# RMS-normed attention and a gated MLP on one core: tokens on 64 lanes of 7 in place of 112 of 4, q and k on the two halves of the partitions, keys in chunks of 128

## The chip, the cores and the metric

The kernel runs on one core of a Trainium2 chip. The time is the device time of one execution in microseconds (us). The core has five engines with a queue each: TensorE (PE in the profile), VectorE (DVE), ScalarE (ACT), GpSimd (POOL) and SyncE (SP, which here only issues transfers). Before the change the median was 428.67 us.

## The reference

```python
q_n, k_n = rmsnorm(q, g_q), rmsnorm(k, g_k)     # 8 batches x 12 heads x 448 tokens x 64
attn = softmax(q_n @ k_n.T / 8)                 # per head
x = (attn @ v).transpose(0, 2, 1, 3)            # -> 3584 tokens x 768
h = x @ w_in                                    # 768 x 2048
out = (h * sigmoid(1.702 * h)) @ w_out          # 2048 x 768
```

## The kernel before

Heads are worked in 48 pairs. For each pair q, k and v are loaded, q and k squared (ACT), summed (DVE), normed (POOL), transposed, scored against each other (TensorE), exponentiated (ACT), multiplied with v (TensorE) and divided (DVE). From the first batch on the two projections of the MLP run in between on TensorE.

In the cuts below "..." marks what is left out, and long names are shortened. The order on every engine is fixed before the run: a list scheduler gets each task with its engine, a planned duration and a priority, and writes out one queue for each engine; each queue then runs in the order written. The priorities of the first pairs were tuned against the planned durations.

```python
# loads: 112 partitions, 4 tokens each; one transfer for q, one for k, one for v
src = (q, k, v)[which][b, h0:h0 + 2].rearrange("h (ss ns) d -> ss h ns d", ns=NS)   # ss = 112
nc.sync.dma_start(out=vraw[turn(i, N_RAW, K_VRAW)][:SS], in_=src)                    # v
eng.dma_start(out=raw[turn(i, N_RAW, K_RAW)][:SS, which], in_=src)                   # q or k
...
# the scheduler's task for a load: 0.46 us of SyncE, 0.9 us of movement
od.add(("L", i, w), "SP", 460, lambda: load(i, w), at - 7 + ...,
       deps=[("N", prior(i, N_RAW, K_RAW), gi) for gi in range(2)], moves=900.0)
...
# scores: 4 chunks of 112 keys, two heads on the two halves of TensorE's rows
for hp in range(2):
    r = slice(64 * hp, 64 * hp + 64)
    nc.tensor.matmul(sc[:, hp, ...], lhsT=qkw[r, k0:k0 + WIN], rhs=qk[r, 0, qs])
# values: 4 matmuls of 65 columns for each head and block of queries
for kc in range(NS):
    nc.tensor.matmul(os_[u, w][:, x, :], lhsT=att[:SS, kc, hp, ...], rhs=vx[:SS, hp, kc, :])
```

## Time and profile before

| | before |
|---|---|
| time, median of 3 | 428.67 us (428.58 to 428.96) |
| span of the profiled run | 426.3 us |
| TensorE busy in the span | 96% |
| TensorE busy from 100 to 370 us | 265.0 of 270 us |
| SyncE: issuing loads, all told | 73.3 us for 143 loads |

The busy shares and the table by stretch are shown in the prediction below.

And two rows of the waits (who waited, for what: total us, times, longest):

```profile
DVE ssq L534 <- ACT sq L525: 9.8, 14, 3.8
ACT sq L525 <- DMA raw<-in_k_dram: 7.0, 7, 1.5
```

### The profile page before, as it was taken

The numbers are of one execution on the slowest core, as the hardware profiler recorded it, in microseconds if no ns is written. First come the engines' busy times: TensorE is split into PE (matmuls) and PEld (weight loads), VectorE is DVE, ScalarE is ACT, GpSimd is POOL, SyncE is SP. The second block draws the span as 40 slices with busy tenths as digits, with TensorE's granted clock in tenths as the row PEclk, the third lists the DMA queues.
The fourth block names the chain that finished last, engine by engine and source line by source line (L and its number), as shares of the span: only waits on it lengthen the run. The fifth ranks groups of instructions, "written<-read, shape, count | busy, mean of one in ns | idle before, by whom it ended". The sixth has DMA issues, their size and how long they took to land.

```text
span 426.3 us, 10048 instructions
## 1 busy us (share of the span) xinstructions
PE 409.1 (96%) x3874; PEld 241.7 (57%) x3874; DVE 297.3 (70%) x584; ACT 302.6 (71%) x437; POOL 189.8 (45%) x277
## 2 busy tenths in 40 slices
PE   6899899999989999999999999999999999999995
PEld 4558686655555555555555555555555555565553
DVE  5967988579988677965787577764676555655663
ACT  4898788869978699978986589867775477604400
POOL 6396853657387473854636355553642100000000
PEclk9999999999999999999999999999999999999999
DMA  8999999575559989667636687556333630121023
GB/s 224 248 257 245 258 246 248 141 161 129 134 124 205 219 196 208 155 166 156 170 103 160 156 227 165 136 136 169 74 77 95 157 90 13 23 67 38 0 75 92
DMA packets 101555, 63.38 MB, mean 149 GB/s; under 512 B 54916, under 2 KB 101508, under 8 KB 101508
## 3 DMA queue, kind: packets, MB, share of 16 engines
q1 hardware_dynamic: 93712, 55.88, 53.9%
q0 software_dynamic: 7296, 6.29, 9.0%
q8 instruction: 30, 0.49, 0.5%
q10 hardware_dynamic: 500, 0.57, 0.4%
q14 instruction: 17, 0.14, 0.1%
HBM read 45.61 MB, written 11.01 MB: 133 GB/s over the span
## 4 chain that ended last, share of the span: by engine, by line
PE 78%; DVE 11%; ACT 5%; issue 3%; DMA 2%; POOL 0%; DVEq 0%
PE w L875 30%; PE w L965 17%; PE o L664 10%; PE sc L643 9%; PE sc L965 4%; PE w L905 4%; DVE late L956 4%; PE sc L875 2%; ACT att L653 2%; ACT sq L525 1%; DVE ssq L534 1%; DVE obs L675 1%; DVE g L897 1%; DMA raw<-in_k_dram 1%; DVE w_out_s L945 1%
## 5 line engine op out<-in xcount | busy, mean ns | idle before, releaser
L651 ACT ACTIVATE att<-sc 112x896 bf16<-112x896 f32 x168 | 145.8, 917 | 33.4 <-PE sc L643 32.9
L875 PE MATMUL w<-xt,w_in_s 128*128 128x448 bf16 (+1 forms) x810 | 150.7, 330 | 0.1
L875 PEld LDWEIGHTS <-w_in_s 128*128 128x128 bf16 x864 | 78.1, 97 | 54.2 <-issue 6.7
L576 POOL TENSOR_TENSOR row<-raw,rs 112x512 bf16<-112x512 f32 x80 | 89.5, 1139 | 25.8 <-DMA qk<-row 13.5
L664 PEld LDWEIGHTS <-att 112*128 112x128 bf16 x1536 | 72.5, 98 | 49.3 <-issue 18.2
L897 DVE SCALAR_TENSOR_TENSOR g<-th,w 128x448 bf16<-128x448 f32 x119 | 72.5, 616 | 26.8 <-ACT th L885 26.3
L885 ACT ACTIVATE th<-w 128x448 f32<-128x448 f32 x119 | 64.6, 548 | 26.3 <-PE w L875 24.7
L664 PE MATMUL o<-vx,att 112*128 112x65 bf16 x1280 | 74.2, 194 | 4.9 <-DVE obs L675 4.7
L589 POOL TENSOR_TENSOR vx<-vraw,ones 112x512 bf16<-112x512 f32 x35 | 36.5, 1042 | 95.0 <-PE o L664 59.4
L534 DVE TENSOR_REDUCE ssq<-sq 112x16 f32<-112x1024 f32 (+1 forms) x50 | 58.5, 1171 | 10.4 <-ACT sq L525 9.8
L525 ACT ACTIVATE sq<-raw 112x1024 f32<-112x1024 f32 (+1 forms) x43 | 44.5, 1036 | 11.2 <-DMA raw<-in_k_dram 7.0
L643 PE MATMUL sc<-qk 64*128 64x448 bf16 (+1 forms) x360 | 46.9, 342 | 1.6 <-DVE qk L606 1.4
L675 DVE TENSOR_TENSOR obs<-o,rcp 112x256 bf16<-112x256 f32 x96 | 40.8, 425 | 3.3
L965 PEld LDWEIGHTS <-g 128*128 128x128 bf16 x336 | 29.9, 97 | 19.6 <-issue 3.0
L674 DVE RECIPROCAL rcp<-o 112x4 f32<-112x4 f32 x96 | 17.1, 178 | 33.0 <-PE o L664 32.4
L965 PEld LDWEIGHTS <-late 128*128 128x128 bf16 x328 | 28.8, 97 | 18.3 <-issue 2.6
L965 PE MATMUL w<-w_out_s,g 128*128 128x384 bf16 x176 | 33.5, 325 | 0.0
L965 PE MATMUL w<-w_out_s,late 128*128 128x384 bf16 x152 | 29.7, 326 | 0.2 <-DVE late L956 0.2
L965 PE MATMUL w<-late 128*128 128x384 bf16 x144 | 28.1, 326 | 0.0
L978 DVE TENSOR_SCALAR osb<-w 128x384 f32<-128x384 f32 x25 | 13.9, 557 | 16.8 <-PE w L965 16.8
L617 ACT ACTIVATE qk<-qk,gG 128x448 bf16<-128x448 bf16 x36 | 24.2, 676 | 0.3 <-DMA qk<-row 0.3
L566 POOL TENSOR_TENSOR t<-rs 112x48 f32<-112x48 f32 x28 | 8.2, 292 | 35.8 <-DVE rs L555 34.7
(92 smaller groups left out, 379.7 us busy)
## 6 DMA issues: line engine op xcount, KB each, us to landing
raw<-in_q_dram SPq DMA_DIRECT2D x44, 224.0 KB, 3.7
raw<-in_k_dram SPq DMA_DIRECT2D x43, 224.0 KB, 4.7
vraw<-in_v_dram SPq DMA_DIRECT2D x42, 224.0 KB, 3.7
w_in_s<-in_moe_w_in_dram POOLq DMA_DIRECT2D x4, 768.0 KB, 15.8
w_out_s<-in_moe_w_out_dram POOLq DMA_DIRECT2D x4, 768.0 KB, 21.2
out_dram<-osb SPq DMA_DIRECT2D x14, 168.0 KB, 2.4
out_dram<-osb SPq DMA_DIRECT2D x12, 144.0 KB, 2.6
out_dram<-osb SPq DMA_DIRECT2D x12, 120.0 KB, 2.5
```

The source lines that it names most:

```text
L525: nc.scalar.activation(out=sq[i % N_SQ][:SS, part], in_=raw[turn(i, N_RAW, K_RAW)][:SS, part], func=ACT.Square)
L534: nc.vector.reduce_sum(out=ssq_of[g0][:SS, i - g0, part], in_=sq[i % N_SQ][:SS, part], axis=AX.X)
L576: eng.tensor_tensor(out=row_ring[i % N_QKN][:SS, gi].rearrange("p n (h d) -> p h n d", h=2), in0=raw[turn(i, N_RAW, K_RAW)][:SS, gi], in1= ...
L589: nc.gpsimd.tensor_tensor(out=vx[:, :, :D], in0=vr, in1=ones[:SS, :].to_broadcast([SS, 2 * NS, D]), op=ALU.mult)
L643: nc.tensor.matmul(sc[:, hp, j * SH:j * SH + n], lhsT=qkw[r, k0:k0 + WIN], rhs=qk[r, 0, qs], start=True, stop=True)
L651: nc.scalar.activation(out=att[:SS, t, :, :S], in_=sc, func=ACT.Exp)
L664: nc.tensor.matmul(os_[u, w][:, x, :], lhsT=att_of(u)[:SS, kc, hp, qs * SS:qs * SS + WIN], rhs=vx_ring[turn(i, N_V, K_V)][:SS, hp, kc, :], ...
L675: nc.vector.tensor_tensor(out=to[:SS, :, w, :] if h is None else to[:SS, :2].rearrange("p n h d -> p (n h) d"), in0=o[:SS, :, :D], in1=rcp ...
L875: nc.tensor.matmul(gps[b, m][:, j * SH:j * SH + n], lhsT=w_in_s[:, ki, f * 128:(f + 1) * 128], rhs=xT[b][:, ki, lo:lo + n], start=(ki == 0 ...
L885: nc.scalar.activation(out=th[:, :], in_=gps[b, m][:, :S], func=ACT.Tanh, scale=0.851)
L897: nc.vector.scalar_tensor_tensor(out=g_of[b // 2][:, f:f + len(g), lo:lo + n], in0=view(ths.pop((b, m))[:, :]), scalar=1.0, in1=view(gps.p ...
L965: nc.tensor.matmul(held[to], lhsT=lhs[:, ko, :], rhs=y[:, ko, :], start=first and ko == 0, stop=ko == NK - 1, skip_group_check=not first)
```

## The change

The intent is to fill the partitions: 448 = 64 x 7, so q takes partitions 0 to 63 and k 64 to 127 of one tile, and squares, sums, norms and transposes work on all 128. Keys become three chunks of 128 for each head and one chunk of 64 keys of either head, kept block-diagonal, so that one of the four exponentials of a pair shrinks by half and for each block of queries the values need one matmul of 130 columns for both heads and three of 65 for each head. v is loaded in two halves, one token twice. The core of the diff (532 changed lines, most of them the table of tuned priorities):

```diff
+    LN, NT, NC = 64, 7, 3                          # lanes, tokens of a lane, chunks of a head
-        src = ....rearrange("h (ss ns) d -> ss h ns d", ns=NS)
+        src = ....rearrange("h (s n) d -> s h n d", n=NT)
-            nc.sync.dma_start(out=vraw[...][:SS], in_=src)
+            for side in range(2):
+                first = 1 - side
+                nc.sync.dma_start(out=to[LN * side:LN * side + LN, first:first + 2 * NC + 2]...,
+                                  in_=src[:, :, NC * side:NC * side + NC + 1]...)
-        eng.dma_start(out=raw[...][:SS, which], in_=src)
+        eng.dma_start(out=raw[...][LN * which:LN * which + LN]..., in_=src...)
...
+    def part_k(i):                                 # the shared chunk, block-diagonal
+        for hp in range(2):
+            nc.gpsimd.tensor_scalar(out=parts_of(i)[2][:, LN * hp:LN * hp + LN],
+                                    in0=turned_k(i)[:, 2 * NC], scalar1=gG2[:, hp:hp + 1], ...)
...
+        for lo in whole:
+            nc.tensor.matmul(sc[:, 0, lo:lo + n], lhsT=apart, rhs=qs, start=True, stop=True)
...
-        while c < (tm + 1) * 128: ...                   # stores of 16 to 112 rows
+        for c in range(tm * 128, (tm + 1) * 128, LN): ...   # stores of 64 rows
...
-                   moves=900.0)
+                   moves=975.0 if w == 2 else 690.0)    # planned movement; SyncE's 460 stays
+            od.add(("KB", i), "POOL", 320, lambda i=i: part_k(i), ...)
```

## The prediction

> **What bounds the kernel now.** I read the busy shares first, then the busy times by stretch, then single instructions on TensorE, then the other engines up to the first projection, then the waits. Times are us from the span's start.
>
> ```profile
> PE 409.1 (96%) x3874; PEld 241.7 (57%) x3874; DVE 297.3 (70%) x584; ACT 302.6 (71%) x437; POOL 189.8 (45%) x277
> ```
>
> The table by stretch has, after each stretch and its length, the busy time of PE, PEld, DVE, ACT and POOL, then granted clock, DMA share and GB/s:
>
> ```profile
> 0.00:10.00 10.00, 6.64 (x46) 4.79 (x47) 5.16 (x13) 4.31 (x8) 5.84 (x28) 1.00 0.87 222
> 10.00:20.00 10.00, 8.19 (x108) 5.26 (x107) 9.82 (x20) 8.08 (x14) 4.75 (x5) 1.00 1.15 250
> ...
> 25.00:30.00 5.00, 4.69 (x62) 2.67 (x59) 1.96 (x6) 4.91 (x7) 5.00 (x5) 1.00 1.16 265
> 30.00:35.00 5.00, 4.77 (x84) 3.12 (x80) 4.03 (x10) 5.00 (x7) 2.46 (x3) 1.00 1.17 249
> 35.00:60.00 25.00, 23.20 (x326) 20.53 (x322) 20.41 (x48) 19.87 (x29) 15.98 (x24) 1.00 1.19 251
> ...
> 100.00:370.00 270.00, 265.04 (x2443) 146.88 (x2440) 189.12 (x366) 211.69 (x304) 127.99 (x177) 1.00 0.60 142
> ```
>
> From 100 to 370, TensorE is 98% busy while ACT and DVE are at 78% and 70%: there only TensorE's own stream counts. Before 35 it is otherwise: DVE is full from 10 to 20, ACT from 20 to 35, DMA saturated near 250 GB/s, and part of TensorE's busy time is warming matmuls on zeros (89, 14.8 us).
>
> The timeline gives the price of one matmul by where the next one starts:
>
> ```profile
> 200.21 1.30 PE L875 MATMUL w<-xt,w_in_s 128*128 128x448 bf16 x6
> 201.34 0.42 PE L664 MATMUL o<-vx,att 112*128 112x65 bf16 x8
> 201.60 1.30 PE L875 MATMUL w<-xt,w_in_s 128*128 128x448 bf16 x6
> 202.83 0.55 PE L643 MATMUL sc<-qk 64*128 64x448 bf16 x4
> 203.31 0.30 PE L664 MATMUL o<-vx,att 112*128 112x65 bf16 x4
> ```
>
> Six of 448 columns take 1.13 (188 ns each), eight of 65 take 0.26 (33 ns each). Four score matmuls on 64 rows take 0.48: they run in pairs, 2 x 189 = 0.38, plus 0.10; another 0.10 is lost before them (201.60 + 6 x 0.188 = 202.73, yet they start at 202.83).
>
> By these prices and the page's counts the stream is: projections 672 x 0.189 + 192 x 0.096 = 145; output products 808 x 0.163 (384 columns) = 132; values 1536 x 0.0335 = 51.5; scores 168 pairs x 0.189 + 48 short pairs x 0.096 = 36; transposes 144 x 0.05 = 7. Sum 372. With 108 groups of scores at 0.2 of switching (21) and some 10 of warmers it makes 403, of the 420.6 from the first matmul at 1.36 to the end of the last at 422.0. So about 18 is waiting. I took the excess over these prices by stretch: most of it lies before 60; from 60 to 370 only some 6 is not switching.
>
> The start is led by the exponentials. The timeline of ACT just before the first projections:
>
> ```profile
> 24.56 7.66 ACT L653 ACTIVATE att<-sc 112x896 bf16<-112x896 f32 x9
> 32.12 1.05 ACT L525 ACTIVATE sq<-raw 112x1024 f32<-112x1024 f32 x1
> 33.06 3.36 ACT L653 ACTIVATE att<-sc 112x896 bf16<-112x896 f32 x4
> 36.49 0.54 ACT L885 ACTIVATE th<-w 128x448 f32<-128x448 f32 x1
> ```
>
> Nine without a gap, 0.85 each, then four more; the first w_in matmul starts at 35.2. The groups that the change touches:
>
> ```profile
> L651 ACT ACTIVATE att<-sc 112x896 bf16<-112x896 f32 x168 | 145.8, 917 | 33.4 <-PE sc L643 32.9
> L664 PE MATMUL o<-vx,att 112*128 112x65 bf16 x1280 | 74.2, 194 | 4.9 <-DVE obs L675 4.7
> L534 DVE TENSOR_REDUCE ssq<-sq 112x16 f32<-112x1024 f32 (+1 forms) x50 | 58.5, 1171 | 10.4 <-ACT sq L525 9.8
> L643 PE MATMUL sc<-qk 64*128 64x448 bf16 (+1 forms) x360 | 46.9, 342 | 1.6 <-DVE qk L606 1.4
> ```
>
> ACT itself waited 33 us for scores: over the whole run it follows TensorE. The largest real wait of TensorE in mid-run is 4.7 us in 7 pieces for the divided outputs (DVE obs), where DVE runs the long additions at the end of a batch.
>
> **What the Trainium skill says.** "TensorE: Matmul & The Clock Gate", section "Wait — 56ns, not 53.3ns?", gives N / 2.4 + about 2.5 ns start to start. The trace agrees at 448 columns (189) and 384 (163); at 65 it would be 29.6 and the trace has 33. "TensorEngine Tiling (Array Packing)", section "Key Properties", says that changing the tiling mode drains TensorE; the two 0.10 us gaps agree. "ScalarE: Activation LUTs", section "What ACT_TABLE_LOAD costs", gives 0.833 ns per element plus a constant; from tanh (448: 548 ns) to exp (896: 917 ns) the trace has 0.824. "SBUF — State Buffer", section "Door 1: The DMA port swizzle (why `[64,N]` ≈ `[32,N]`)", says that partitions 0 to 63 reach only 8 of 16 ports; no transfer of before has that shape, so no run shows it yet.
>
> **The change part by part.**
>
> TensorE. Scores were four pairs per two heads; they become three pairs plus one full-row matmul of block-diagonal keys, again four times 189 ns. The groups, and so the switches, stay 108. Values fall from 1536 of 65 columns to 1152 of 65 and 192 of 130 (130 / 2.4 + 2.5 = 57 ns, an estimate by the page above): 38.6 + 10.9 = 49.5, **2.0 us less**, all on the path. Transposes go from 96 of 112 columns to 84 of 128: equal.
>
> ACT. Of 168 wide exponentials 42 shrink to 448 elements (about 548 ns): 42 x 0.37 = 15.5. Of the 24 early ones 12 shrink to 672 (estimate 0.917 - 224 x 0.824 = 0.73): 2.2. 44 squares go from 1024 to 896 elements, -0.107 each: 4.6. Scaling, 448 to 384 elements x 36: 1.9. Together 24 us of 302.6, but beside TensorE's stream and so worth nothing after 60.
>
> DVE. 46 reductions go from 1214 to about 1079 ns (1.05 ns an element, from the 512 and 1024 forms): -6.2. Each early K copy becomes three instructions (444 ns to about 850, x 12) and each early V cast four (675 to about 1050, x 5): +6.7. Even in total, but early pairs get about 0.3 us dearer just where DVE is full. POOL: the second norm drops to 384 elements (-9), but V is split in two (+9) and 72 small key scalings come in, 12 to 26 us: from 45% to about 50%.
>
> DMA. q and k move in packets of 1792 bytes for 1024, 256 packets a pair for 448; v reads one token twice, 256 for 224. In the trace an undisturbed 1024-byte packet takes 46 ns and a 1536-byte one 65, so 1792 would take 75 (estimate): q and k 7% cheaper, v 14% dearer, together even.
>
> The start. The built program's order has 18 exponentials before the first projection's tanh (9 of each size) where before has 20. 20 x 0.85 = 17.0 against 9 x 0.85 + 9 x 0.67 = 13.7: 3.3 sooner. Given back: 0.3 to 0.5 for the longer chain to the first keys, and one attention unit (values 0.5, scores 0.4) now done after the first projection. I count **2.5 us**; the order also has 76 warmers for 89. From 35 to 75 the shorter exponentials help a stage where ACT is at 79% and TensorE loses 1.8 of 25: **1 us**. The waits at batch ends may shrink with the shorter reductions and the new order: **1 us**. Sum 2.0 + 2.5 + 1 + 1 = 6.5: 428.7 - 6.5 = **422 us**.
>
> **The rivals.** (a) DVE takes the start over from ACT: 9.82 of 10 busy from 10 to 20 speaks for it, 1.96 of 5 from 25 to 30 against. The 2.5 falls to nothing: 424.5. (b) A transfer holds the first projections. The w_in chunks took 11.8 to 19.1 us to land and share a saturated DMA with loads that now write half of the partitions; if those run slower, as the port section suggests, w_in or the late pairs come late: 425 to 428. Against it: packets are larger, and q and k alternate between the halves. (c) The new order removes most of the 6 us of mid-run waits and more of the start: 416 to 418. (d) The key scalings on POOL, between its 1 us operations, delay scores: 424 to 428; against it, POOL idles half of the time.
>
> **Range and chances.** The certain part is 2.0; the rest depends on a reshuffled order, worth some 4 us either way, more by (b). Range 417 to 427. Faster by 2% means under 420.1 and needs (c): 0.3. Slower by 2% needs (b) and (d) together: 0.02. Within 2%: 0.68.
>
> **What would show it.** Right: values' starts 33 ns apart plus 57 for the wide ones; score groups still 0.48 with 0.10 before; 42 exponentials near 550 ns; ACT near 278 busy; first w_in matmul near 32.5; the stretch 100 to 370 still 98% busy. Wrong: a first w_in matmul at 35 or later with DVE or a w_in transfer before it (a, b); score groups that switch more often or cost more; PE under 96% in mid-run with KB or POOL as the releaser (d).

## More of the kernel before

The chain of work that ended last, by engine as shares of the span:

```profile
PE 78%; DVE 11%; ACT 5%; issue 3%; DMA 2%; POOL 0%; DVEq 0%
```

It is a TensorE chain; transfers and SyncE hold 2% of it.

The squares hardly wait for their loads: the transfers run well ahead.

## The result, and the profile after

| | before | after |
|---|---|---|
| median | 428.81 us (4 runs) | **446.04 us** (445.09 to 447.65, 4 runs) |
| ratio | | 1.0406, 95% interval 1.0375 to 1.0437: slower |
| profiled span | 426.3 us | 444.3 us |

Ratios here and below are the mean time of one kernel's runs over that of the other's of the same rounds, so not quite the ratio of the medians quoted.

The busy shares of the changed kernel:

```profile
PE 412.8 (93%) x3603; PEld 246.3 (55%) x3603; DVE 293.3 (66%) x629; ACT 277.6 (62%) x435; POOL 223.8 (50%) x395
```

ACT fell by 25 us and POOL rose to 50%, as predicted. TensorE's busy time didn't fall; it counts matmuls that wait inside the pipeline or run at a lower clock (below). By stretch (columns as in the prediction):

```profile
0.00:10.00 10.00, 6.74 (x30) 4.21 (x30) 3.62 (x19) 3.71 (x8) 5.06 (x26) 1.00 0.82 177
10.00:20.00 10.00, 6.97 (x70) 4.96 (x71) 8.23 (x25) 6.55 (x12) 7.84 (x10) 1.00 1.13 238
...
35.00:60.00 25.00, 22.20 (x304) 18.73 (x301) 21.83 (x60) 17.13 (x26) 16.64 (x23) 1.00 1.19 251
100.00:370.00 270.00, 254.45 (x2159) 143.11 (x2158) 177.11 (x354) 183.36 (x285) 154.32 (x271) 0.99 0.71 145
```

Two places lose. From 10 to 20 every engine but POOL does less than before (TensorE started 70 matmuls for 108). From 100 to 370 TensorE is 94% busy, where it was 98%, and did 2159 matmuls for 2443 (the new program has 7% fewer in all, not 12%). The chain that ended last now reads:

```profile
PE 53%; DMA 14%; DVE 12%; POOL 7%; SPq 6%; issue 4%; ACT 3%; DVEq 0%; POOLq 0%; ACTq 0%
```

DMA and SyncE's queue (SPq) went from 2% to 20%. The waits say where:

```profile
POOL qk L690 <- DMA qk<-row: 48.1, 18, 5.3
ACT att L732 <- PE sc L720: 40.9, 27, 3.3
ACT sq L562 <- DMA raw<-in_k_dram: 35.0, 15, 4.9
...
DVE ssq L571 <- ACT sq L562: 33.4, 25, 4.7
```

Squares wait 35.0 us for k's load, where it was 7.0, and the sums 33.4 for the squares, where it was 9.8. A piece of the chain in mid-run, in order of time (start, us, what):

```profile
187.16 2.25 POOL row L619 x2
...
189.43 0.65 SPq L554
...
190.14 5.05 DMA raw<-in_k_dram
...
195.30 0.96 ACT sq L562
...
197.49 0.43 DVE obs L767
...
197.97 0.23 PE o L754
```

This is a loop: a norm (row) frees a load buffer, the load goes out, the square waits for it, DVE's queue stands still until its sum can start, and the division (obs) that TensorE needs stands behind that sum. Of its 10.8 us, 5.05 lie between the issue of k's load and its landing; "Rate or issue" below tests what that means. In the kernel before, the chain of the same stretch has only TensorE and DVE in it, and 6% of issue.

A part of the loss comes on top of the waiting. In the tables by stretch the third figure from the end is the clock that TensorE was granted. Here are the 3.4 us up to the end of that loop, and the 3.4 us after it:

```profile
194.80:198.20 3.40, 1.26 (x13) 0.62 (x11) 1.78 (x5) 2.90 (x5) 0.85 (x2) 1.00 0.96 202
198.20:201.60 3.40, 3.40 (x21) 1.67 (x18) 0.60 (x2) 2.78 (x5) 2.63 (x9) 0.50 0.83 225
```

TensorE was busy for 1.26 of 3.4 us, and then had half its clock for 3.4 us. The changed kernel's trace has three such stretches before its last matmul (from 20.7, 198.2 and 317.6 us), and in the 3.4 us ahead of each TensorE was busy for 1.3 to 1.8 us; the trace of before has none. If all the work in them took twice its time, they cost 3 x 1.7 = 5.1 us, so up to 5 of the 17 us come by this way (an estimate). The mean clock of every run: 0.981 to 0.988 for the changed kernel, 0.994 to 1.0 for the one before. No experiment separates this part from the waits that come before it.

Why should loads be late? SyncE's queue at the same time, before and after (start, us, line, transfer, count):

```profile
195.40 0.53 SPq L515 DMA_DIRECT2D vraw<-in_v_dram  x1
195.98 0.45 SPq L518 DMA_DIRECT2D raw<-in_q_dram  x1
196.48 0.45 SPq L518 DMA_DIRECT2D raw<-in_k_dram  x1
```

```profile
195.38 1.26 SPq L548 DMA_DIRECT2D vraw<-in_v_dram  x2
196.69 0.60 SPq L554 DMA_DIRECT2D raw<-in_k_dram  x1
197.38 1.19 SPq L1020 DMA_DIRECT2D out_dram<-osb  x2
198.68 0.65 SPq L554 DMA_DIRECT2D raw<-in_q_dram  x1
```

A pair's three loads took 1.43 us of SyncE's time before; now they are four and take 2.5. All issues on SyncE together, transposes and stores included, went from 216.7 to 284.1 us. The issue records of the whole trace, by rows of the transfer, show what is odd about it. Median issue time on SyncE:

| rows of the transfer | 16 | 32 | 48 | 64 | 80 | 96 | 112 |
|---|---|---|---|---|---|---|---|
| stores, kernel before (14 to 16 of each) | 422 ns | 418 | 415 | **568** | 413 | 417 | 402 |
| loads, kernel before | | | | | | | 450 ns (lowest 312) |
| loads, changed kernel | | | | **605 ns** (lowest 595) | | | |

The trace of the kernel before had it already: only stores of 64 rows were slow to issue. The change makes every load and every store one of 64 rows.

### The profile page after: what moved, and what is told of

It is laid out like the page before. It is cut to its first block, busy times and chain, and to the rows that moved or that the text cites. A ratio compares the mean times of both kernels' runs of the same rounds, so it can differ in the third digit from the quotient of the medians.

```text
span 444.3 us, 9718 instructions
## 1 busy us (share of the span) xinstructions
PE 412.8 (93%) x3603; PEld 246.3 (55%) x3603; DVE 293.3 (66%) x629; ACT 277.6 (62%) x435; POOL 223.8 (50%) x395
## 2 busy tenths in 40 slices
DMA packets 94643, 64.93 MB, mean 146 GB/s; under 512 B 55684, under 2 KB 94596, under 8 KB 94596
## 4 chain that ended last, share of the span: by engine, by line
PE 53%; DMA 14%; DVE 12%; POOL 7%; SPq 6%; issue 4%; ACT 3%; DVEq 0%; POOLq 0%; ACTq 0%
PE w L973 18%; PE w L1057 12%; DMA raw<-in_k_dram 8%; PE o L757 5%; PE sc L720 4%; PE sc L1057 4%; POOL row L619 4%; DVE ssq L571 3%; PE w L1003 2%; PE sc L973 2%; DMA late<-in_v_dram 2%; SPq L548 2%; PE sc L723 2%; PE o L754 2%; DVE late L1048 2%
## 5 line engine op out<-in xcount | busy, mean ns | idle before, releaser
L732 ACT ACTIVATE att<-sc 128x896 bf16<-128x896 f32 (+1 forms) x168 | 130.6, 826 | 41.1 <-PE sc L720 40.9
L619 POOL TENSOR_TENSOR row<-raw,rs 128x512 bf16<-128x512 f32 (+1 forms) x82 | 79.1, 985 | 3.0 <-ACT rs L582 2.6
L571 DVE TENSOR_REDUCE ssq<-sq 128x14 f32<-128x896 f32 (+1 forms) x50 | 52.1, 1045 | 33.7 <-ACT sq L562 33.4
L641 POOL TENSOR_TENSOR vx<-vraw,v_of_head 128x256 bf16<-128x256 f32 x70 | 44.1, 646 | 54.2 <-PE o L757 33.2
L757 PEld LDWEIGHTS <-att 128*128 128x128 bf16 x1152 | 61.3, 99 | 16.9 <-issue 0.4
L757 PE MATMUL o<-vx,att 128*128 128x65 bf16 x960 | 65.4, 195 | 0.0
L690 POOL TENSOR_SCALAR qk<-qk,gG 128x64 bf16<-128x64 bf16 x72 | 36.5, 521 | 48.3 <-DMA qk<-row 48.1
L562 ACT ACTIVATE sq<-raw 128x896 f32<-128x896 f32 (+1 forms) x42 | 38.8, 928 | 35.1 <-DMA raw<-in_k_dram 35.0
L754 PE MATMUL o<-vx,att 128*128 128x130 bf16 x160 | 35.9, 225 | 6.9 <-DVE obs L767 6.8
L720 PE MATMUL sc<-qk 64*128 64x448 bf16 (+1 forms) x270 | 39.6, 349 | 0.8 <-DVE qk L667 0.6
L754 PEld LDWEIGHTS <-att 128*128 128x128 bf16 x192 | 18.8, 98 | 31.2 <-issue 10.7
## 6 DMA issues: line engine op xcount, KB each, us to landing
vraw<-in_v_dram SPq DMA_DIRECT2D x84, 128.0 KB, 3.3
late<-in_v_dram SPq DMA_DIRECT2D x12, 128.0 KB, 9.4
```

What stands on the lines that cost most here:

```text
L571: nc.vector.reduce_sum(out=ssq_of[g0][:, i - g0, part], in_=sq[i % N_SQ][:, part], axis=AX.X)
L619: eng.tensor_tensor(out=row_ring[i % N_QKN][:, gi:NT:2].rearrange("p n (h d) -> p h n d", h=2), in0=raw[turn(i, N_RAW, K_RAW)][:, :, ns], ...
L641: nc.gpsimd.tensor_tensor(out=vx[:, n, :D], in0=vr[:, 1 + NC * hp:2 + NC + NC * hp], in1=v_of_head[:, n].to_broadcast([128, NC + 1, D]), o ...
L720: nc.tensor.matmul(sc[:, hp, lo:lo + n], lhsT=ks[r, c * WIN:(c + 1) * WIN], rhs=qs[r], start=True, stop=True)
L732: nc.scalar.activation(out=o, in_=sc[:, :, :S] if t < NC else sc[:, 0, :S], func=ACT.Exp)
L754: nc.tensor.matmul(o[:, x:x + 2, :], lhsT=att_of(u)[:, NT - 2, qs * SS:qs * SS + WIN], rhs=vx[:, NC:NC + 2, :], start=True, stop=True)
```

## The experiments

All comparisons are with the kernel before on the same chip, whose medians were 428.3 to 428.8 us. "Order kept" means that what the scheduler was told is unchanged, so each engine gets its tasks in the same order. SyncE's time for loads, where given, is the sum of the issue records of the run's trace.

### First theories: GpSimd's key scalings, and the bytes of the loads

**e1_kb_act**: the scalings of the shared chunk go to ScalarE.

```diff
     def scale_k(i):
         nc.scalar.activation(out=..., in_=turned_k(i)[:, :2 * NC], func=ACT.Identity, scale=gG)
+        for hp in range(2):
+            nc.scalar.activation(out=parts_of(i)[2][:, LN * hp:LN * hp + LN], ...,
+                                 scale=gG2[:, hp:hp + 1])
     def part_k(i):
-        for hp in range(2): nc.gpsimd.tensor_scalar(...)
+        pass
```

> Two theories for the 17 us. K: the two small key scalings on GpSimd (521 ns each for an expected 160 to 370, and 48 us of waiting in line for the transposed rows) delay the normalisations, and with them the loads and everything behind. L: the loads onto 64 partitions land later than the order was built for, so squares block ScalarE in its queue. Here the scalings are done by ScalarE next to the other key scaling, in the same order of everything else. K expects most of the loss in mid-run to go: 430 to 435 us, and ScalarE's wait for raw keys under 15 us (35 in the changed kernel). L expects little: 443 to 448 us, with that wait still near 30 us. ScalarE gains about 72 x 0.33 = 24 us of work either way.

Correct, 445.79 us (2 runs), ratio 1.0404. GpSimd's busy share fell to 43%, the time didn't move. On GpSimd the scalings had cost 521 ns each instead of my estimated 160 to 370, but they aren't what holds the kernel.

**e2_short_loads**: q and k of pairs from 7 on bring 4 of 7 tokens.

```diff
+        nn = NT if i < N_RAW else 4
-        eng.dma_start(out=raw[...]..., in_=src...)
+        eng.dma_start(out=raw[...][..., :nn]..., in_=src[:, :, :nn]...)
```

> Wrong result on purpose. From the eighth pair on, q and k loads bring 4 of 7 tokens (the rest of the buffer is old data): same number of transfers and same 64 partitions, packets of 1024 bytes for 1792, same order. L expects 428 to 436 us, because the transfers land about 0.5 to 1 us sooner and ScalarE's wait for raw keys falls under 15 us. K expects 442 to 447 us: the loads are late because GpSimd frees their buffers late.

Wrong, 450.01 us (448.9 and 451.11), ratio 1.0503. Moving 56.87 MB in place of 64.93 did not help. The test was weaker than I thought: in its trace SyncE still took 0.605 us to issue each short load, and alone on the chip (form g below) a transfer of that shape still took 0.68 us.

**e3_both**: both edits.

> Both edits of the two runs before, wrong result on purpose. If K and L each carry a part, this is the fastest of the three: 422 to 430 us. If only one of them does, it is within 2 us of that one. If neither, above 440 us: then the cause lies in the first 60 us or in the static order itself.

Wrong, 444.97 us (441.77 and 448.17), ratio 1.0385. Neither theory stands in the form tested: the number and the shape of the transfers had stayed.

**e4_loads_alone**: a program of nothing but loads, 12 pairs in each of seven forms (a: the three loads of before; b: the four of after; c, d: q and k of before and of after; e: 128 partitions x 1792 bytes; f: as d with k on ScalarE's queue; g: v of after).

> Wrong result on purpose (zeros). Only the loads of 12 pairs, in seven stretches one after the other: a) q, k, v as before (112 partitions, 1024-byte packets); b) as changed (q and k onto 64 partitions each in 1792-byte packets, v as two halves); c) q and k as before; d) q and k as changed; e) q and k in 1792-byte packets over all 128 partitions; f) as d, but k issued by ScalarE; g) v as changed. If partitions 0 to 63 reach only half of the ports, d runs at about 200 GB/s and e at 300 or more, and f lies between; if only the packet size matters, d and e are equal and both faster than c by some 7 per cent. If the issue by the SP queue (0.6 us a transfer) binds, b takes 12 x 4 x 0.6 = 29 us or more.

| form | c: 112 rows x 2 x 1024 B | d: 64 rows x 2 x 1792 B | e: 128 rows x 1792 B | f: d on two queues | g: 64 rows x 2 x 1024 B |
|---|---|---|---|---|---|
| us between landings (mean after the first six) | 0.83 | 0.965 | 0.595 | 0.95 | 0.68 |
| SyncE's issue, ns | 313 | 605 | 340 | 600 | 605 |
| one packet, ns (median) | 66 | 129 | 74 | 126 | 46 |

A transfer of 229 KB to 64 partitions moves at 238 GB/s, to 128 at 385, to 112 at 276; a packet of the same 1792 bytes takes 129 ns for 74. The section "Door 1" cited in the prediction says that 64 partitions reach half of the ports, and the trace agrees in kind: 238 GB/s for 385. The scheduler had been told 0.69 us. And an issue takes twice as long. Two suspects were left, the rate and the issue.

### The loads taken out of the way

**e5_wide_loads** and **e8_wide_kb**: each of q, k and v comes in one transfer of 128 partitions (the wrong data, the right amount); e8 also has e1's edit. Order kept.

```diff
-        src = ....rearrange("h (s n) d -> s h n d", n=NT)
+        src = ....rearrange("h (s n) d -> (h s) (n d)", n=NT)
-            for side in range(2): nc.sync.dma_start(out=to[LN * side:...], ...)     # v
+            nc.sync.dma_start(out=vraw[...][:, 1:1 + NT]..., in_=src)
-        eng.dma_start(out=raw[...][LN * which:LN * which + LN]..., in_=src...)
+        eng.dma_start(out=raw[...][:, which]..., in_=src)
```

> The changed kernel in its own order, with q, k and v each brought by one transfer of 128 partitions of 1792 bytes in place of two transfers of 64 partitions (q, k) and two half transfers (v). Wrong result on purpose, everything after the loads unchanged. Alone on the chip a 64-partition transfer took 0.60 us of SyncE's queue and 0.965 us to move, a 128-partition one 0.34 and 0.595; a pair's loads 2.42 us of issue and 2.91 of movement now, 1.02 and 1.79 here. Theory W (the loads' cost, issue and rate, is what the static order was not built for): 416 to 425 us, squares no longer wait for the load. Theory P (POOL's scalings, transposes and stores matter as much): 427 to 438. Theory O (the order itself is worse, whatever the loads cost): 440 or more.

> The wide loads of the first run and also the key scalings of the shared chunk on ScalarE instead of GpSimd; wrong result on purpose. With the loads out of the way this shows what GpSimd's scalings cost: theory W alone says the same as the first run within 2 us; theory P says 4 us or more below it.

Fast runs of e5: 435.71, 437.09 and 439.18, ratio 1.0204; of e8: 433.45, 435.19 and 439.11, ratio 1.0171. The profiled run of e5 took 809.86 us with every TensorE stretch about twice as long at a recorded clock of 1.0; I can't explain it and leave it out. About half of the loss was back, less than theory W said. e8's profile (a run 1.5% above its fastest, so only single instructions are read from it) shows why. Two stretches of VectorE on its chain:

```profile
17.87 2.60 DVE late L631
...
53.56 5.56 DVE late L631
```

These are copies of 64 x 64 values in the value cast, 0.19 us each when nothing is in the way. Here GpSimd worked without a pause from 53.45 on, and a copy begun at 53.56 ended at 59.1. "SBUF — State Buffer", section "SBUF: two separate sides", says that VectorE and GpSimd share a port pair as an exclusive lock for certain VectorE operations; the trace agrees in kind, with 5.56 us as the price here, over several GpSimd instructions in a row. In the changed kernel itself the ten copies cost under 2 us beyond 0.19 each.

**e9_wide_nolock** and **e11_wide_nolock_kb**: e5 and e8 with these copies written as sums of one element, as the kernel does for the other three tokens.

```diff
-                nc.vector.tensor_copy(out=vx[mine, NC + hp, :D], in_=vr[mine, NC + 1])
+                nc.vector.reduce_sum(out=vx[mine, NC + hp, :D], axis=AX.X,
+                                     in_=vr[mine, NC + 1].rearrange("p (d o) -> p d o", o=1))
```

> The wide loads once more (wrong result on purpose), with the value cast's two 64-partition copies on VectorE written as sums of one element, as the three-token part beside them is. With the wide loads alone three of these copies had met work on GpSimd in the first 60 us and took 1.65, 2.60 and 5.56 us in place of 0.19, which cost about 9 us that the changed kernel itself doesn't pay. Theory W: without them 422 to 431 us, the first pairs on time. If something else in the start or the middle costs as much as the loads do: 434 or more.

> Wide loads, no copies that meet GpSimd, and the scalings of the shared chunk on ScalarE: all costs that the plan had too low are gone but the stores. Theory W with the rest: 417 to 428 us, and at most 4 us below the run without the move to ScalarE. If it stays above 432, the loads and GpSimd together don't make the loss.

e9: wrong, **426.47 us** (425.28 to 428.83), ratio 0.9954 (0.9911 to 0.9996). e11: 428.12, ratio 0.9985. With the loads cheap the changed kernel is 19.6 us faster than with its own, and no scaling on GpSimd needs to move for it. Its 110 stores are still of 64 rows, so those alone do no such harm. But these loads are cheaper than those of the kernel before too (66.5 us of SyncE's time for 73.3), so e9 is a lower bound and not a fair version of the change. e9's mid-run and its squares:

```profile
100.00:370.00 270.00, 266.14 (x2285) 151.04 (x2284) 184.73 (x372) 194.84 (x302) 155.10 (x274) 1.00 0.60 139
```

```profile
ACT sq L556 <- DMA raw<-in_k_dram: 12.1, 10, 2.3
```

TensorE is back at 98.6%, and the squares' wait fell from 35.0 to 12.1.

### Rate or issue

**e10_wide_issue**: e9 with two tiny transfers of 64 rows after each v; **e13_wide_32rows**: the same with 32 rows.

```diff
+            for side in range(2):
+                nc.sync.dma_start(out=spare[(2 * i + side) % len(spare)][:64],   # e13: [:32]
+                                  in_=some[:, :, side:side + 1])                 # e13: [:32]
```

> As the run before it, with two small transfers of 64 partitions and two runs of 4 bytes after each pair's v: the issue time on SyncE goes back up (1.02 us of a pair to about 2.2, against 2.42 in the changed kernel) while nearly no bytes are added. If the issue time is what hurts: 6 us or more above the run before it. If the rate of the transfers is: within 3 us of it.

> As the run with wide loads and two small transfers of 64 rows a pair, with 32 rows in each small transfer, whose issue took 0.31 us alone in place of 0.605. Wrong result on purpose. The number of transfers is the same. If the number is what hurts: 450 us or more, as with 64 rows. If the time of the issues is: about half way between 426.5 and 453.9, 433 to 445.

e10: 453.9 us, ratio 1.0578. Transfers of 512 bytes each, 27 us slower than e9, and the mid-run looks like the changed kernel's:

```profile
100.00:370.00 270.00, 249.83 (x2108) 140.02 (x2107) 175.43 (x345) 179.47 (x279) 151.93 (x268) 0.98 0.65 139
```

The rate of the transfers does not explain it, as the times from issue to landing show:

| | q, k: median us from issue to landing | squares' wait for k's load, us |
|---|---|---|
| before | 3.7, 4.7 | 7.0 |
| changed kernel | 4.6, 4.9 | 35.0 |
| e9 | 3.5, 4.0 | 12.1 |
| e10 | 3.2, 3.8 | 35.3 |

In e10 a load, once issued, lands no later than in e9; yet the squares wait as long as in the changed kernel, because the loads go out later: SyncE's queue waited 27.1 us for norms to free a load's buffer in e9 and 8.5 in e10, so it came to the loads when their buffers had mostly been free for some time. So it is the issue, not the rate. e13: 436.89, 440.83 and 442.83 us, ratio 1.0276, with as many transfers as e10 and 13 us less. Its spread is wide (the fastest of the three had the highest granted clock, 0.992 for 0.982 and 0.984), but it has 239 loads where the changed kernel has 191 and is not slower than that: the number alone is not it.

**e7_before_split**: the kernel before, each load split at partition 64, correct, order kept.

```diff
-        eng.dma_start(out=raw[...][:SS, which], in_=src)
+        for lo, hi in ((0, 64), (64, SS)):
+            eng.dma_start(out=to[lo:hi], in_=src[lo:hi])
```

> The kernel before in its own order, each load split into a transfer of partitions 0 to 63 and one of 64 to 111: the same bytes, correct results, only the loads dearer on SyncE and in movement, as in the change. Theory W: 436 us or more, with squares that wait for the load as in the changed kernel. Rivals, for which the loads are not the cause: 428 to 431.

Correct, 462.75 us, ratio 1.0801, and its squares wait 35.6 us for k. The packets of its main queue took no longer than before (49.4% of 459.6 us for 53.9% of 426.3), so here too it is not the rate. The old body with twice the issues, half of them of 64 rows, is slower than the new one. Set against SyncE's time for loads, the runs whose order was kept line up (the changed kernel also has the copies, worth under 2 us):

| kernel | loads | SyncE issuing loads, us | time, us |
|---|---|---|---|
| e9_wide_nolock | 143 | 66.5 | 426.5 |
| e13_wide_32rows (issuing read from its profiled run, 446.6 us, slow) | 239 | 116.6 | 440.8 |
| changed kernel | 191 | 123.4 | 446.0 |
| e10_wide_issue | 239 | 135.6 | 453.9 |
| kernel before | 143 | 73.3 | 428.7 |
| e7_before_split | 286 | 178.0 | 462.8 |

One us more of issuing costs 0.34 us of time from e9 to the changed kernel (19.5 / 56.9), 0.40 to e10 (27.4 / 69.1), 0.29 to e13 (14.3 / 50.1), and 0.33 from before to e7 (34.1 / 104.7); e1 to e3, with 124.7 to 128.0 us of issuing and 445.0 to 450.0 us, fall in with these. The lower clock is part of these prices (e10's runs had 0.963 to 0.981, e9's 0.995 to 0.996). "DMA: Bandwidth & Descriptors", section "Issuing engines are not separate DMA queues", says that the time to initiate a transfer is usually small relative to the transfer; here it was 0.605 us against 0.965, and it was what counted.

**e12_issue_forms**: loads alone, eight of each count of rows.

> Loads alone, eight of each form one after the other, to read the time of one issue on SyncE from the trace (wrong result on purpose). In the kernel before, stores of 64 rows already took 568 ns to issue and those of 16, 32, 48, 80, 96 and 112 rows 402 to 422. If the count of exactly 64 rows is what makes an issue slow: near 0.31 us for 32 to 63 and 65 to 112 rows of two heads, 0.60 for 64. If small partition counts are slow: 0.60 for all up to 64. If a 64-row issue costs the same for four heads as for two, 0.60 for both, loads of two pairs at once would halve it.

| rows, two heads | 32 | 48 | 56 | 60 | 63 | 64 | 65 | 66 | 72 | 80 | 96 | 112 |
|---|---|---|---|---|---|---|---|---|---|---|---|---|
| median issue, ns | 312 | 429 | 398 | 417 | 352 | **605** | 390 | 369 | 393 | 442 | 449 | 456 |

Of the counts that could be read, 64 alone is slow, on either half of the partitions; one head of 64 rows took 595 and four heads 615 to 618. With 62 and 68 rows SyncE stalled later in the series, up to 3.4 us an issue, so their medians say nothing of the issue itself. An issue close behind one of 64 rows is slow as well: e7's 48-row halves took 592 ns (median of 128) straight after one of 64 rows, and 350 (of 15) where there was a gap. Why 64 is slow no run tells.

### Can the order give it back?

The scheduler was told 0.46 us for a load of q, k or v, so its order may simply be made for another machine.

**e6_honest_plan**: the changed kernel, told the measured costs, old priorities.

```diff
-            od.add(("L", i, w), "SP", 460, ..., moves=975.0 if w == 2 else 690.0)
+            od.add(("L", i, w), "SP", 1240 if w == 2 else 620, ..., moves=1360.0 if w == 2 else 965.0)
-            od.add(("KB", i), "POOL", 320, ...)
+            od.add(("KB", i), "POOL", 1090, ...)
```

> The changed kernel with correct results, where the scheduler is told what runs showed: SyncE 0.62 us for q or k and 1.24 us for v (0.46 each before), 0.965 and 1.36 us of movement (0.69 and 0.975), 1.09 us for the key scalings on GpSimd (0.32). Its own plan then ends at 439 us, where the plan with the old costs ended at 416. Theory W says that the plan is kept within 4 us: 437 to 444 us. If the harm were only in an order built for other costs, ordering anew would give it back: under 430.

Correct, 444.83 us, ratio 1.0381: hardly a gain. Its plan had said 439.

**e14_retuned**, **e15_pairs_retuned** and **e16_tuned_old_costs**: priorities searched anew by small random changes of the plan; e14 for measured costs, e15 for loads of two pairs in one issue from pair 8 on, e16 as a control with the old costs.

```diff
 KEYS, AT, ON = ...                                   # all three: new tables
-        src = (q, k, v)[which][b, h0:h0 + 2]...
+        src = (q, k, v)[which][b, h0:h0 + nh]...      # e15, e18: nh = 4 from pair 8 on
```

> The changed kernel with correct results; only the order is new. The scheduler's priorities were searched again with 0.645 us of SyncE for q and k and 1.26 for v, 0.965 and 1.0 us of movement, and 0.95 us for the key scalings; its plan then ends at 426.2 us, with no idle TensorE left between 100 and 400 us. Theory: the issue time cost 17 us because the order was made for another; then 427 to 433 us. If 64-row issues cost it in any order: 440 or more.

> Correct results. From pair 8 on one transfer of 64 rows brings q, k or a half of v of two pairs (four heads), so that SyncE issues half as often; the order was searched for it and its plan ends at 424.9 us. 425 to 431 us; at best 1 per cent under the kernel before.

> Control for the re-tuned order: the changed kernel, its priorities searched again in the same way but with the old costs (0.46 us of SyncE for a load); its plan ends at 414.7 us. Correct results. If it is the right issue time that helps and not the search: 440 us or more, as the changed kernel.

All correct: 449.04, 450.93 and 439.04 us (ratios 1.0479, 1.0515, 1.0249). e14 and e15 missed badly. Their search had been free to move value casts to VectorE: e14 has 46 of the 64-partition copies for 10, eight of them 0.76 to 1.68 us long, and VectorE at 74%. They are confounded and settle nothing.

**e17_retuned_no_moves** and **e18_pairs_no_moves**: the same two searches with every task left on its engine and the copies written as sums.

> Changed kernel, correct results: priorities searched again for the measured issue times, with every task left on the engine that it had, and the value cast's copies written as sums of one element. Its plan ends at 425.6 us. If the order is what the issue time spoils: 427 to 434 us. If 64-row issues cost their time in any order: 438 or more.

> The same, with the loads of two pairs in one issue from pair 8 on (half the issues); its plan ends at 425.7 us. If the issue time hurts in any order, this one is 4 us or more below the run before it; if the order was all, equal to it within 3 us, and 426 to 433 us.

Both correct: 440.03 us (ratio 1.028) and 436.75 (1.0181). e17 keeps TensorE 98% busy from 100 to 370, yet gains only 6 us on the changed kernel. That is no better than the control (439.04, itself a us under what I had expected), which knew nothing of the true issue times. So both searches gave 6 to 7 us, whichever costs they were told. e18 has half the load issues from pair 8 on, 77.1 us of SyncE's time for 122.2, and is another 3.3 us faster, a little less than the 4 that were expected of an effect in any order. No correct version beat the kernel before.

But neither comparison is clean. The control was free to move norms and squares between engines and kept the copies. And e17 has an accident of its own, on the chain of its trace:

```profile
54.79 6.36 DVE L1166 TENSOR_TENSOR row<-raw,rs 128x384 bf16<-128x384 f32 x1
```

This norm on VectorE took 0.55 us the two other times; here GpSimd worked from 53.3 to 60.7 without a pause. TensorE waited 5.4 us for a division behind it, and its clock, halved at 54.6, stayed so to 68.3 (8.2 us busy). Without both (5.8 us of the norm, up to 4.1 of clock) e17 would come to some 430 us, by estimate; e18 has no such norm (its longest took 1.18 us). So whether an order made for the true issue times could give the loss back is not shown either way.

## Why the prediction was wrong

It said 422 us, 417 to 427; the kernel took 446.0. Step by step:

- **TensorE's stream: right.** Starts of values are 32 ns apart, those of the wide ones 58; a score group of four still takes 0.49. By the prediction's prices the stream with warmers fell by some 4 us (381.9 to 377.9), of which 13 fewer warmers are 1.4.
- **ACT: right.** 277.6 us busy for 278 predicted; the 42 short exponentials take 538 ns for 548, the early ones 725 for 730.
- **POOL: share right, term mis-sized.** 50% as said; but the 72 scalings took 36.5 us for 12 to 26. e1 and e11 show that this costs nothing.
- **DMA: the step that failed.** "q and k 7% cheaper, v 14% dearer, together even" scaled the packet's time by its bytes, from packets to 112 partitions. Alone on the chip, packets of 1792 bytes to 64 partitions took 129 ns for the estimated 75, and a pair's loads 2.91 us for 2.48. Worse, the step counted only movement. It never priced the issue: 605 ns each and four for a pair, where three took 450. It also held that no transfer of before had the shape of 64 partitions; 16 stores had. e10 shows that issue time alone is enough for the loss; e9, that with cheap loads the kernel lands at 426.5, within the range, though with loads cheaper than the prediction's "even".
- **The start: wrong sign, by the same step.** The 2.5 us were to come from shorter exponentials. The first matmul with w_in started at 36.9, later than the 35.1 of before, not near 32.5: the first scores came at 14.5 for 10.7, behind loads that landed later. Here the rate counts too: the first k load, issued at 0.75 us for 0.77, landed at 5.34 for 4.55. With the wide loads of e9 the first matmul with w_in started at 32.8, as forecast.
- **Mid-run: the assumption failed.** The work beside TensorE was "worth nothing after 60"; so I looked at engines with slack and never at SyncE, whose queue is in order. From the first matmul to the last TensorE took 38.8 us beyond the prices before and 60.6 after; some 15 of the 22 added lie after 60 us.
- **Rivals.** (b) came nearest, with the port section behind it, but it was kept to w_in and the first 60 us and given 425 to 428. (d) had the wait on transposes and GpSimd (48.1 us in the waits), and e1 shows that it isn't the cause. (a) did not come either: DVE was busy for 8.23 of 10 us from 10 to 20, less than before. Nor did (c).

What is shown: more time of SyncE's queue in issuing makes a loss of this size in this order, by e9 against e10, and by e7 in the old body. In the changed kernel itself issue and rate were not separated (e9 makes both cheap), and giving some of the loads to another engine's queue was not tried there. What stays open: why 64 rows are slow to issue; whether a fitting order would give the loss back (the best found left 8 to 12 us of it, e17's with its long norm); how much of it is the lower clock; and some 4 us between e9 and the 422 predicted.

## What to carry to other kernels

Price a transfer twice, its movement and the time its issue takes on the queue of the engine that starts it, and read the second from the trace by shape before changing a shape: 16 stores of the old kernel already showed that 64 rows are dear. An engine that only issues has no busy share on the page, yet its queue is in order like any other. A test that cuts bytes but keeps the number and shape of the transfers tests only the bytes. And before two runs are compared, look in both for a single instruction of many times its usual length, and at the granted clock: here 6.36 us for 0.55, and 13.7 us at half clock around it, sat in the run that was to decide about the order.

## What the Trainium skill lacked or had wrong

- "DMA: Bandwidth & Descriptors": no word that the issue time on SyncE depends on the count of rows. Measured: 605 ns at 64 rows, 312 to 456 at 32, 48, 56, 60, 63, 65, 66, 72, 80, 96 and 112, for the same two runs of 1024 bytes a row.
- The same page, section "Issuing engines are not separate DMA queues": "usually small relative to the DMA itself" does not hold here; 0.605 us of issue against 0.965 of movement, and 0.29 to 0.40 us of run time for each us of issue added.
- "SBUF — State Buffer": no word that a VectorE instruction may wait for several GpSimd instructions in a row. Measured: a copy of 0.19 us took 5.56 (e8), a norm of 0.55 us took 6.36 (e17).
- No page gives the time of so small a scaling on GpSimd: 128 x 64 values of bf16 took 521 ns in the mean, about 440 undisturbed.
